# Talking-heads attention: one two-bank PSUM tile for a period's two pre-mixes, and one VectorE maximum over both

## Chip, cores and metric

The kernel runs on one core of one Trainium2 chip. The metric is device time in microseconds (us), from the start of the program to its end. Shown are the median of three runs of the kernel before, and one more execution that was profiled.

## What is computed

Three stages follow each other: an attention in which the heads are mixed before and after the softmax, and two feed-forward layers. The change lies in the attention.

```python
# q, k, v: 4 batches, 12 heads, 448 tokens, head size 64
scores = scale * np.matmul(q, k.transpose(0, 1, 3, 2))
scores = np.einsum('bhij,hg->bgij', scores, w_pre)          # pre-mix of the heads
scores = scores - np.max(scores, axis=-1, keepdims=True)
attn = np.exp(scores)
attn = attn / (np.sum(attn, axis=-1, keepdims=True) + 1e-09)
attn = np.einsum('bhij,hg->bgij', attn, w_post)             # post-mix of the heads
attn_out = np.matmul(attn, v)
# then two feed-forward layers over 1792 tokens: 768 -> 1024 -> 768 and 768 -> 2048 -> 768
```

## The kernel before

**Blocks and periods.** The queries of each batch are cut into chunks of 120 or 88 tokens, and each chunk into blocks of up to ten queries. A block holds its queries times twelve heads on the partitions and the 448 keys along the free dimension. There are 180 blocks; two neighbours make a period, so there are 90 periods, `s` = 0 to 89.

**The way of one block.** `qk` (line L222) makes scores with TensorE, in a ring of PSUM tiles of two banks each (two buffers), and ScalarE copies them to an SBUF tile `ssrc` (L229). `shuffle` (L236) is a DMA that gathers a block's rows into `sdst`. `pre` (L256) mixes the heads: per period two blocks, each into a PSUM tile of its own of one bank (`ps_pre`, four buffers: two periods' worth). `negmax` (L267) lets VectorE find the negated maximum of each row, per block. `expo` (L274) lets ScalarE compute the exponential with that maximum as bias, per block, and its row sum into `sm`. `weigh` (L284, L285, L287) is three GpSimd operations for a period: reciprocals of the sums, multiplied into the post-mix weights `w`. `post` (L307) mixes and transposes with TensorE into the same ring as `qk`; `post_out` (L337) copies that to `at` with VectorE. `av` (L373) multiplies by V into the ring, and ScalarE copies it out (L379, L391, L394).

**The order.** It is written out by hand: a loop over `s` issues in each step `pre(s+2)`, `post_out(s-1)`, the `qk` jobs of the step, `negmax` and then `expo` of period `s+2`, the `av` jobs, `weigh(s+1)`, and `post(s)`. Every engine runs its share strictly in that order. Between them stands the narrowing of the first layer's weights, spread over all engines (L82 to L103, L440). In the last steps of the attention no `qk` is left, and the loop instead begins to load the first layer's weights (`wraw`, three buffers), which ScalarE rounds (L477) and from which GpSimd takes the remainder (L478). The first layer's products (L490) follow.

Of the kernel before, what the change touches and what calls it, by code (L numbers as in the profile page):

```python
# [7 lines left out]
F32 = mybir.dt.float32  # L8
# [3 lines left out]
AF = mybir.ActivationFunctionType  # L12
ALU = mybir.AluOpType
AX = mybir.AxisListType
# [4 lines left out]
def kernel(  # L19
# [16 lines left out]
    nc = tc.nc  # L36
    B, D, _ = qT.shape
    H = w_pre.shape[0]
    S = v.shape[1]
# [15 lines left out]
    scale = 1.0 / float(D) ** 0.5  # L55
# [65 lines left out]
    late_p = late.__enter__()  # L121
# [111 lines left out]
    def shuffle(t):  # L233
        c, f, nk, r, oa = blocks[t]
        d = gaps[t % 10]
        (nc.scalar if t % 2 and t < 12 else nc.sync).dma_start(out=d[4:4 + r * H], in_=ssrc[c][f:f + (r - 1) * nk + 1:nk])  # L236
        sdst[t] = d

    def size(t, g):

        return RH if g == 0 else blocks[t][3] - RH

    es = {}
    sms = {}
    pres = {}
    nms = {}
    ws = {}

    def pre(s):

        ps = [psb_p.tile([128, 512], F32, tag="pre", name="ps_pre", bufs=4) for b in range(2)]
        ds = [sdst.pop(2 * s + b) for b in range(2)]
        for b, r in ((0, 0), (0, 1), (1, 0), (1, 1)):
            u = r ^ b
            m = H * size(2 * s + b, 1) if r else 64
            nc.tensor.matmul(  # L256
                out=ps[b][64 * u:64 * u + 64, 0:S],
                lhsT=wpre_bd[64 * r:64 * r + m],
                rhs=ds[b][64 * r:64 * r + m],
                start=True,  # L260
                stop=True,
            )
        pres[s] = ps

    def negmax(s, b):
        nm = late_p.tile([128, 1], F32, tag="nm", name="nm", bufs=6)
        nc.vector.tensor_reduce(out=nm, in_=pres[s][b][:, 0:S], op=ALU.max, axis=AX.X, negate=True)  # L267
        nms[s, b] = nm

    def expo(s, b):  # L270
        e = late_p.tile([128, S], F32, tag="e", name="e", bufs=6)
        if b == 0:
            sms[s] = late_p.tile([128, 2], F32, tag="sm", name="sm", bufs=4)
        nc.scalar.activation(  # L274
            out=e, in_=pres[s][b][:, 0:S], func=AF.Exp, bias=nms.pop((s, b)), scale=1.0, accum_out=sms[s][:, b:b + 1]
        )
        es[s, b] = e
        if b:
            pres.pop(s)

    def weigh(s):

        sm = sms.pop(s)
        nc.gpsimd.tensor_scalar(out=sm, in0=sm, scalar1=1e-9, scalar2=None, op0=ALU.add)  # L284
        nc.gpsimd.tensor_tensor(out=sm, in0=sm, in1=eps_sb[:, 2:3].to_broadcast([128, 2]), op=ALU.pow)  # L285
        w = late_p.tile([128, 2, H, RH], F32, tag="w", name="w", bufs=3)
        nc.gpsimd.tensor_tensor(  # L287
            out=w.rearrange("p b g i -> p b (g i)"),
            in0=wpost_bd.rearrange("p g i -> p (g i)").unsqueeze(1).to_broadcast([128, 2, H * RH]),
            in1=sm.unsqueeze(2).to_broadcast([128, 2, H * RH]),  # L290
            op=ALU.mult,
        )
        ws[s] = w
# [31 lines left out]
    def post_out(s):  # L325
        pv = pps.pop(s)[:, :, 0:NU * RH].rearrange("p u (n i) -> p u n i", i=RH)
        (c0, _, _, _, k0), (c1, _, _, _, k1) = [blocks[2 * s + b] for b in range(2)]
        for c in (c0, c1):
            if c not in at:
                at[c] = late_p.tile([128, NU, PH], F32, tag="at", name="at", bufs=2)  # L330
                nk = sorted(chunks[c]["nks"])
                if nk[0] != nk[1]:
                    t = at[c].rearrange("p n (u x) -> p n u x", u=2)
                    nc.vector.memset(t[:, :, :, RH * nk[0]:RH * nk[1]], 0.0)
        def put(c, k, h, n0, n1):
            dst = at[c][h, n0:n1].rearrange("p n (u x) -> p u n x", u=2)
            nc.vector.tensor_copy(dst[:, :, :, RH * k:RH * k + RH], pv[h, :, n0:n1])  # L337

        if c0 == c1:
            assert k0 == k1  # L340
            put(c0, k0, slice(0, 128), 0, NU)
        else:
            for b, (c, k) in enumerate(((c0, k0), (c1, k1))):
                put(c, k, slice(0, 128), b * NJ * H, b * NJ * H + NJ * H)
                put(c, k, slice(64 * b, 64 * b + 64), 2 * NJ * H, NU)
# [70 lines left out]
    def load_w1(i):  # L416
        src, dst, k, o = w1pieces[i]
        t = raw_p.tile([128, WP], I64, tag="w1raw", name="w1raw", bufs=7)
        nc.gpsimd.dma_start(out=t, in_=src[k * 128:(k + 1) * 128, o:o + WP])
        w1raw[i] = t  # L420
# [10 lines left out]
    def start_w1(i):  # L431
        part = narrow_w1(i)
        next(part)
        fill.append(part)
# [69 lines left out]
    def half_line(pool, n=8):  # L504

        nc.vector.memset(pool.tile([128, n], F32, name="pad"), 0.0)
# [60 lines left out]
    psb_p = psb.__enter__()  # L567


    DS, DP = 5, 2  # L570
# [6 lines left out]
    for c, ch in enumerate(chunks):  # L577
        if c:
            beg = (chunks[c - 1]["first"] + 1) // 2 - DS
            end = ch["first"] // 2 - DS  # L580
            for p in range(HP):
                rest = end - beg >= HP
                s = beg + rest + p * (end - beg - rest) // HP
# [24 lines left out]
    for s in range(lo_s, NP + 2):  # L608
        js = jobs.pop(s, [])
        for kind in (load_k, load_q, load_v, load_const):  # L610
            for f, a in js:
                if f is kind:
                    f(*a)
        if 0 <= s + DS < NP:
            shuffle(2 * (s + DS))
            shuffle(2 * (s + DS) + 1)
        ready = sorted(w1t)
        scales = sorted(w1s)
        for f, a in js:
            if f is x_out and s < NP:  # L620
                f(*a)
        if first_w1 <= s:
            room += share - moved.get(s, 0)
        while room >= 384 and owed < len(w1pieces):
            room -= 384
            owed += 1
        for _ in range(2):
            if len(w1at) < owed and len(w1at) - kept < 7:
                load_w1(len(w1at))
                w1at.append(s)  # L630
        new = 0 <= s + DP < NP
        if new:
            pre(s + DP)
        if 0 <= s - 1 < NP:
            post_out(s - 1)
        for f, a in js:
            if f is qk:
                f(*a)
        for b in range(2):
            if new:  # L640
                negmax(s + DP, b)
        for b in range(2):
            if new:
                expo(s + DP, b)
        for f, a in js:
            if f is av:
                f(*a)
        if 0 <= s + 1 < NP:
            weigh(s + 1)
        while begun < len(w1at) and w1at[begun] <= s - 3 and len(fill) + len(w1f) < 4:  # L650
            start_w1(begun)
            begun += 1
        for i in scales:
            scale_w1(i)
        for i in sorted(w1f):
            sq, t = w1f.pop(i)
            flush(sq, t)
            w1s[i] = t
        for _ in range(7 if any(f is av for f, a in js) else 0):
            filler()  # L660
        if 0 <= s < NP:
            post(s)
        if s >= NP:
            for f, a in js:
                if f is x_out:
                    f(*a, nc.scalar)
        for i in ready:
            store_w1(i)
        kept = begun - len(fill)
        if last_raw is None and kept == len(w1pieces) and not w1t and not w1s and not w1f:  # L670
            last_raw = s
            assert s < last_qk, s
            raws.__exit__(None, None, None)
            wi1 = tc.tile_pool(name="wi1", bufs=1, side="left", reuse_waits="tile")
            wi1_p = wi1.__enter__()
            half_line(wi1_p)
            prep = prep_first()
        if s == last_qk:
            early.__exit__(None, None, None)
            sspools[0].__exit__(None, None, None)  # L680
            wi1b = tc.tile_pool(name="wi1b", bufs=1, side="left", reuse_waits="tile")
            wi1b_p = wi1b.__enter__()
        if s + DP == NP - 1:
            psb.__exit__(None, None, None)
            psh = tc.tile_pool(name="psh", bufs=1, side="left", space=PSUM, reuse_waits="tile")
            psh_p = psh.__enter__()
            h10 = h1(0)
        if last_raw is not None and last_raw < s <= min(last_qk, last_raw + 3):
            next(prep)
        if s > last_qk:  # L690
            for _ in range(1 if s < NP - DS else 2):
                next(prep, None)
        if s in (NP - 2, NP - 1):
            next(h10)
            next(h10)
        if s == NP:
            run(prep)
            run(h10)
# [706 lines left out]
```

## Time and profile before

| what | value |
|---|---|
| median of three runs | 1093.68 us (1092.14 to 1096.95) |
| the profiled execution, whole / its span | 1091.86 us / 1090.1 us |
| TensorE busy, of the span | 1031.3 us (95%) |
| VectorE busy | 678.5 us (62%) |
| ScalarE busy | 561.7 us (52%) |
| GpSimd busy | 672.9 us (62%) |

The span is that of the profile, from the first instruction to the last; 1.8 us of the execution's own time lie around it. A share of busy time is a mean over stages: the attention ends near 392 us, and all else is feed-forward layers.

### The profile page before, as it was taken

Reading aid. Unit: us, or ns where it says so; the run is one execution under the profiler, and the core shown is the slowest. Engines: PE = TensorE matmul, PEld = TensorE weight load, DVE = VectorE, ACT = ScalarE, POOL = GpSimd, SP = SyncE. Lnnn points to the kernel's source line nnn. Section 1 sums busy time; section 2 is a strip of 40 time slices with the busy share of each in tenths; the row PEclk is TensorE's granted clock in tenths of the full one; section 3 lists DMA queues with packets and bytes.
Section 4 is the critical chain, followed back from the end, with each engine's and each line's share of the span. In section 5 each row is a group of like instructions: output and inputs, shape, how many; then the busy total and the mean of one; then the engine's idle time right before and its main releaser. Section 6 shows DMA issues by size and latency. Waiting matters only on the chain.

```text
span 1090.1 us, 30147 instructions
## 1 busy us (share of the span) xinstructions
PE 1031.3 (95%) x12220; PEld 884.1 (81%) x12220; DVE 678.5 (62%) x1131; ACT 561.7 (52%) x1195; POOL 672.9 (62%) x868
## 2 busy tenths in 40 slices
PE   7798887998999799999999999999999999999998
PEld 3466555665666688898999989999999999999998
DVE  2577765885776435888887435777646833444444
ACT  4677655786777435443443446344434555444432
POOL 4667986898765726656555158676535757666630
PEclk9999999999999999999999999999999999999999
DMA  8778887889765624556564646445545521111102
GB/s 230 211 213 251 250 231 224 254 244 255 221 205 178 182 71 138 175 180 200 163 200 128 216 140 189 138 143 155 185 163 194 192 102 59 58 59 59 58 29 102
DMA packets 115914, 181.06 MB, mean 166 GB/s; under 512 B 24224, under 2 KB 87200, under 8 KB 115776
## 3 DMA queue, kind: packets, MB, share of 16 engines
q1 hardware_dynamic: 100276, 127.79, 38.2%
q0 software_dynamic: 12608, 48.55, 14.8%
q10 hardware_dynamic: 2892, 2.80, 0.9%
q8 instruction: 96, 1.57, 0.6%
q14 instruction: 42, 0.34, 0.1%
HBM read 102.42 MB, written 38.14 MB: 129 GB/s over the span
## 4 chain that ended last, share of the span: by engine, by line
PE 52%; POOL 4%; issue 3%; DVE 2%; DMA 2%; ACT 1%; SPq 0%; POOLq 0%; ACTq 0%
PE ps_y L1218 19%; PE ps_h L1147 16%; PE ps_o L801 9%; PE ps_h L490 7%; POOL ti L1075 1%; DMA ra<-w2iD 1%; DMA w2oD<-nt 1%; PE ps_tr L787 1%; POOL s L1055 1%; POOL to L1083 1%; DVE st L760 0%; DVE e L757 0%; ACT e L754 0%; DVE nm L751 0%; POOL w1o L727 0%
## 5 line engine op out<-in xcount | busy, mean ns | idle before, releaser
L1218 PE MATMUL ps_y<-to,gt 128*128 128x384 f32 x1332 | 241.8, 336 | 2.6 <-POOL to L1083 1.8
L1218 PEld LDWEIGHTS ps_y<-to,gt 128*128 128x128 f32 x1332 | 233.6, 188 | 4.9 <-POOL to L1083 2.1
L1147 PE MATMUL ps_h<-xc,ti 128*128 128x448 f32 x1080 | 225.1, 362 | 0.6 <-ACT h L1163 0.6
L1147 PEld LDWEIGHTS ps_h<-xc,ti 128*128 128x128 f32 x1080 | 201.6, 188 | 13.2 <-ACT h L1163 1.0
L337 DVE COPY at<-ps_ring 128x840 f32<-128x840 f32 (+2 forms) x114 | 96.1, 854 | 100.7 <-PE ps_ring L307 100.6
L307 PEld LDWEIGHTS ps_ring<-w,e 60*64 60x64 f32 x5040 | 89.0, 136 | 64.9 <-issue 27.3
L1229 DVE TENSOR_TENSOR y<-ps_y,y 128x768 f32<-128x768 f32 x97 | 92.4, 954 | 77.9 <-PE ps_y L1218 77.2
L841 POOL TENSOR_SCALAR nt<-nt 128x256 f32<-128x256 f32 x96 | 111.6, 1163 | 46.0 <-ACT nt L840 40.1
L307 PE MATMUL ps_ring<-w,e 60*64 60x60 f32 x5040 | 98.7, 222 | 27.1 <-issue 14.1
L229 ACT COPY ssrc<-ps_ring 128x896 f32<-128x896 f32 x92 | 82.3, 908 | 81.1 <-PE ps_ring L222 70.7
L274 ACT ACTIVATE e<-ps_pre,nm 128x448 f32<-128x448 f32 x180 | 113.2, 640 | 19.2 <-DVE nm L267 18.5
L801 PE MATMUL ps_o<-zt,w1o 128*128 128x384 f32 (+1 forms) x720 | 120.6, 326 | 1.8 <-ACT o L809 1.6
L490 PE MATMUL ps_h<-w1i,xs 128*128 128x512 f32 x504 | 118.8, 393 | 0.7 <-POOL xs L741 0.6
L801 PEld LDWEIGHTS ps_o<-zt,w1o 128*128 128x128 f32 x720 | 116.9, 189 | 2.5 <-ACT o L809 1.9
L490 PEld LDWEIGHTS ps_h<-w1i,xs 128*128 128x128 f32 x504 | 94.3, 189 | 20.6 <-POOL xs L741 1.5
L1075 POOL TENSOR_TENSOR ti<-ra,ti 128x384 fp32r<-128x384 f32 x56 | 60.0, 1079 | 79.7 <-ACT ti L1074 79.0
L267 DVE TENSOR_REDUCE nm<-ps_pre 128x1 f32<-128x448 f32 x180 | 103.2, 614 | 9.6 <-PE ps_pre L256 8.9
L1160 DVE TENSOR_TENSOR gt<-h,gt 128x448 fp32r<-128x448 f32 x64 | 50.2, 785 | 90.0 <-ACT gt L1165 85.4
L222 PE MATMUL ps_ring<-k,q 64*64 64x448 f32 x752 | 95.9, 561 | 7.8 <-DMA q<-in_qT_dram 3.2
L840 ACT ACTIVATE nt<-nraw 128x256 f32<-128x256 f32 x96 | 41.0, 433 | 119.4 <-DMA w2iD<-nt 29.9
L256 PE MATMUL ps_pre<-sdst,wpre_bd 64*64 64x448 f32 (+1 forms) x720 | 91.9, 547 | 3.1 <-issue 2.8
L1083 POOL TENSOR_TENSOR to<-ro,to 128x768 fp32r<-128x768 f32 x32 | 61.1, 1916 | 45.7 <-ACT to L1082 45.1
(111 smaller groups left out, 1526.3 us busy)
## 6 DMA issues: line engine op xcount, KB each, us to landing
sdst<-ssrc SPq DMA_DIRECT2D x166, 210.0 KB
nraw<-in_moe_w_in_dram SPq DMA_DIRECT2D x48, 256.0 KB
nraw<-in_moe_w_out_dram SPq DMA_DIRECT2D x48, 256.0 KB
ra<-w2iD POOLq DMA_DIRECT2D x32, 384.0 KB, 4.5
ro<-w2oD POOLq DMA_DIRECT2D x32, 384.0 KB, 4.0
w1raw<-in_moe_w_in_dram POOLq DMA_DIRECT2D x24, 256.0 KB, 6.5
w1raw<-in_moe_w_out_dram POOLq DMA_DIRECT2D x24, 256.0 KB, 6.9
w2iD<-nt SPq DMA_DIRECT2D x48, 128.0 KB
```

The lines of the kernel that those rows point to most:

```text
L222: nc.tensor.matmul(out=ps[64 * u:64 * u + 64, e, 0:S], lhsT=qq[c][64 * e:64 * e + 64, p * n + u * half:p * n + u * half + 64], rhs=k[64 * ...
L256: nc.tensor.matmul(out=ps[b][64 * u:64 * u + 64, 0:S], lhsT=wpre_bd[64 * r:64 * r + m], rhs=ds[b][64 * r:64 * r + m], start=True, stop=True,)
L267: nc.vector.tensor_reduce(out=nm, in_=pres[s][b][:, 0:S], op=ALU.max, axis=AX.X, negate=True)
L274: nc.scalar.activation(out=e, in_=pres[s][b][:, 0:S], func=AF.Exp, bias=nms.pop((s, b)), scale=1.0, accum_out=sms[s][:, b:b + 1])
L307: nc.tensor.matmul(out=ps[64 * c:64 * c + 64, u, i0:i0 + PR], lhsT=ee[b][64 * u:64 * u + m, o:o + 64], rhs=w[64 * u:64 * u + m, b], start= ...
L337: nc.vector.tensor_copy(dst[:, :, :, RH * k:RH * k + RH], pv[h, :, n0:n1])
L490: nc.tensor.matmul(out=ps[:, u], lhsT=t[:, a, cc], rhs=w1i[cc][:, w, u * 512:(u + 1) * 512], start=(cc == 0 and a == 0 and w == 0), stop=( ...
L801: nc.tensor.matmul(out=ps[:, 0:width], lhsT=w1o[k][:, w, cc * 128:(cc + 1) * 128], rhs=zT[:, a, k, 0:width], start=(k == 0 and i == 0), st ...
L841: nc.gpsimd.tensor_scalar(out=t, in0=t, scalar1=2.0**-30, scalar2=2.0 - 2.0**-23, op0=ALU.is_ge, op1=ALU.mult)
L1147: nc.tensor.matmul(out=bank[b][:, 0:HT], lhsT=t[:, w, c], rhs=xc[xn][:, a, c], start=(first and j == 0 and c == 0 and i == 0), stop=(j == ...
L1218: nc.tensor.matmul(out=ps[:, u - u2[0], 0:DM // 2], lhsT=gt[:, a, f, o:o + 128], rhs=w[:, v, f, u * (DM // 2):(u + 1) * (DM // 2)], start= ...
L1229: nc.vector.tensor_tensor(out=yo, in0=po, in1=yo, op=ALU.add)
```

## The change

The two pre-mix results of a period go into one tile of two banks, in a pool of two such tiles instead of four of one bank. One VectorE operation reduces both banks, to a tile of two columns, and each exponential takes its column. The matmuls, the exponentials and all other operations stay as they are and in the same places.

```diff
-        ps = [psb_p.tile([128, 512], F32, tag="pre", name="ps_pre", bufs=4) for b in range(2)]
+        ps = psb_p.tile([128, 2, 512], F32, tag="pre", name="ps_pre", bufs=2)
...
-                out=ps[b][64 * u:64 * u + 64, 0:S],
+                out=ps[64 * u:64 * u + 64, b, 0:S],
...
-    def negmax(s, b):
-        nm = late_p.tile([128, 1], F32, tag="nm", name="nm", bufs=6)
-        nc.vector.tensor_reduce(out=nm, in_=pres[s][b][:, 0:S], op=ALU.max, axis=AX.X, negate=True)
-        nms[s, b] = nm
+    def negmax(s):
+        nm = late_p.tile([128, 2], F32, tag="nm", name="nm", bufs=4)
+        nc.vector.tensor_reduce(out=nm, in_=pres[s][:, :, 0:S], op=ALU.max, axis=AX.X, negate=True)
+        nms[s] = nm
...
-            out=e, in_=pres[s][b][:, 0:S], func=AF.Exp, bias=nms.pop((s, b)), scale=1.0, accum_out=sms[s][:, b:b + 1]
+            out=e, in_=pres[s][:, b, 0:S], func=AF.Exp, bias=nms[s][:, b:b + 1], scale=1.0, accum_out=sms[s][:, b:b + 1]
...
-        for b in range(2):
-            if new:
-                negmax(s + DP, b)
+        if new:
+            negmax(s + DP)
```

No instruction changes its place; what each waits for does. On ScalarE, in the middle of the attention, a step before the change reads (`e` is the exponential's output, the names in brackets are the engines and DMA queues waited for):

```order
L229 COPY ssrc<-ps_ring 128x2x448 [waits PE_49]
L274 ACTIVATE e,sm<-ps_pre,nm 128x448 [waits DVE_49,Pool_49]
L274 ACTIVATE e,sm<-ps_pre,nm 128x448 [waits DVE_49]
L379 COPY xt<-ps_ring 128x3x2x6x5 [waits PE_49]
L379 COPY xt<-ps_ring 128x3x2x6x5
```

and after it, in such a step:

```order
L229 COPY ssrc<-ps_ring 128x2x448 [waits PE_49]
L274 ACTIVATE e,sm<-ps_pre,nm 128x448 [waits DVE_49,Activation_49,Pool_49]
L274 ACTIVATE e,sm<-ps_pre,nm 128x448 [waits Activation_49]
L380 COPY xt<-ps_ring 128x3x2x6x5 [waits PE_49]
L380 COPY xt<-ps_ring 128x3x2x6x5
```

The second exponential no longer waits for VectorE, and the first waits for the one operation that gives both maxima. Each also names ScalarE's own earlier exponential in the same of six `e` buffers, three periods back.

On TensorE, at the pre-mix of the third period (`sdst_102` and `sdst_103` are its two blocks), the first that takes PSUM a second time, the difference is:

```order
-L256 MATMUL ps_pre<-sdst_102,wpre_bd 64x448 [waits DMAHW5_49,PE_49,Activation_49]
+L256 MATMUL ps_pre<-sdst_102,wpre_bd 64x448 [waits DMAHW5_49,DVE_49,Activation_49]
 L256 MATMUL ps_pre<-sdst_102,wpre_bd 64x448
-L256 MATMUL ps_pre<-sdst_103,wpre_bd 64x448 [waits DMAHW0_49,PE_49,Activation_49]
+L256 MATMUL ps_pre<-sdst_103,wpre_bd 64x448 [waits DMAHW0_49]
 L256 MATMUL ps_pre<-sdst_103,wpre_bd 64x448
```

The first block's matmul now waits for both exponentials of two periods before, where each block waited for its own.

## Rows read from the trace of the kernel before

**Rows 1.** Busy us of each engine in two stretches, (x) instructions.

```profile
core 0: us, PE busy (x) PEld busy (x) DVE busy (x) ACT busy (x) POOL busy (x), PEclk, DMA share, GB/s
20.00:344.00 324.00, 287.01 (x7407) 192.22 (x7399) 227.78 (x410) 223.70 (x545) 241.82 (x437) 0.98 0.78 229
392.00:1090.00 698.00, 688.95 (x3725) 652.94 (x3724) 425.77 (x679) 309.33 (x583) 392.17 (x360) 1.00 0.43 136
```

**Rows 2.** What TensorE waited for, 20 to 392 us: total us, times, longest us.

```profile
PE ps_ring L307 <- issue: 14.1, 10, 3.1
PE ps_ring L307 <- POOL w L287: 10.4, 10, 3.6
PE ps_ring L373 <- ACT ssrc L229: 10.4, 4, 3.8
...
PE ps_ring L222 <- DVE at L337: 2.5, 3, 1.6
```

**Rows 3.** Groups, 0 to 400 us: count | busy us, mean ns | idle before, releasers.

```profile
L267 DVE TENSOR_REDUCE nm<-ps_pre 128x1 f32<-128x448 f32 x180 | 103.2, 614 | 9.6 <-PE ps_pre L256 8.9 <-issue 0.2
...
L229 DVE COPY ssrc<-ps_ring 128x896 f32<-128x896 f32 x2 | 2.2, 1092 | 9.9 <-PE ps_ring L222 9.9
...
L751 DVE TENSOR_REDUCE nm<-ps_h 128x1 f32<-128x1024 f32 x1 | 1.2, 1224 | 12.1 <-DMA xD<-xt 12.1
```

**Rows 4.** What ScalarE waited for, 20 to 392 us.

```profile
ACT e L274 <- DVE nm L267: 18.5, 16, 2.9
...
ACT ssrc L229 <- DMA sdst<-ssrc: 5.8, 2, 3.5
```

**Rows 5.** What VectorE waited for, 20 to 392 us.

```profile
DVE nm L267 <- PE ps_pre L256: 8.9, 6, 4.2
```

**Rows 6.** Timeline of a quick period: start us, us, instruction, [idle before, releaser].

```profile
102.20 0.94 PE L256 MATMUL ps_pre<-sdst,wpre_bd 64*64 64x448 f32 x8
...
103.40 1.15 DVE L267 TENSOR_REDUCE nm<-ps_pre 128x1 f32<-128x448 f32 x2
...
103.96 0.91 ACT L229 COPY ssrc<-ps_ring 128x896 f32<-128x896 f32 x1 [1.67 <-PE ps_ring L222]
...
104.76 0.64 ACT L274 ACTIVATE e<-ps_pre,nm 128x448 f32<-128x448 f32 x1
...
106.84 0.99 PE L256 MATMUL ps_pre<-sdst,wpre_bd 64*64 64x448 f32 x8
```

**Rows 7.** Timeline of the first period of a chunk, where ScalarE waits for the maximum.

```profile
303.00 1.16 DVE L267 TENSOR_REDUCE nm<-ps_pre 128x1 f32<-128x448 f32 x2
...
303.66 0.63 ACT L274 ACTIVATE e<-ps_pre,nm 128x448 f32<-128x448 f32 x1 [1.45 <-DVE nm L267]
...
305.14 0.98 PE L222 MATMUL ps_ring<-k,q 64*64 64x448 f32 x8 [0.18 <-DVE at L337]
305.22 1.89 ACT L229 COPY ssrc<-ps_ring 128x896 f32<-128x896 f32 x2
...
306.17 0.75 PE L373 MATMUL ps_ring<-at,v 128*64 128x100 f32 x12
```

**Rows 8.** Timeline of the third period's pre-mix and the exponential before it.

```profile
23.93 0.63 ACT L274 ACTIVATE e<-ps_pre,nm 128x448 f32<-128x448 f32 x1
...
24.23 1.07 PE L256 MATMUL ps_pre<-sdst,wpre_bd 64*64 64x448 f32 x6
```

**Rows 9.** Timeline of the last steps, where the first layer's weights are rounded.

```profile
346.04 0.63 ACT L274 ACTIVATE e<-ps_pre,nm 128x448 f32<-128x448 f32 x1 [0.88 <-DVE nm L267]
...
347.27 0.61 ACT L477 CAST w1i<-wraw 128x512 fp32r<-128x512 f32 x1
...
347.96 1.28 POOL L478 TENSOR_TENSOR w1i<-wraw,w1i 128x512 fp32r<-128x512 f32 x1 [1.24 <-ACT w1i L477]
...
350.41 0.39 POOL L287 TENSOR_TENSOR w<-wpost_bd,sm 128x120 f32<-128x120 f32 x1
...
350.85 1.24 PE L307 MATMUL ps_ring<-w,e 60*64 60x60 f32 x53 [0.23 <-POOL w L287]
```

More of the change, by code (lines that the diff above doesn't have):

```diff
@@ L279, in expo @@
             pres.pop(s)
+            nms.pop(s)
     def weigh(s):
```

## The prediction

> **What bounds the kernel now.** I read the busy time by stretch first [rows 1]. From 392 us to the end TensorE is busy 688.95 of 698 us: that part has no room, and nothing of the change runs in it. It only starts earlier or later. So whatever the change does, it does to the moment at which the attention hands over. In the attention's main stretch, 20 to 344 us, TensorE is busy 287.01 of 324 us, GpSimd 241.82, VectorE 227.78 (70%), ScalarE 223.70, with the DMA engines at 0.78. No engine but TensorE is near full, and TensorE loses 37 us.
>
> The table of what TensorE waited for says where [rows 2]: 14.1 us inside the post-mix with no releaser the profile can name, 10.4 us for GpSimd's weights `w`, 10.4 us for ScalarE's copies of scores, and 2.5 us, in three waits, for VectorE's copy `at`. The reduction that the change touches does not stand there by name. It can reach TensorE in three ways: through VectorE's queue (the copy `at` behind it frees a ring buffer), through ScalarE (the exponential, behind which copies of scores free ring buffers), and through the exponential and GpSimd to `w`.
>
> **The reduction itself.** Before, 180 reductions take 103.2 us of VectorE, which is 103.2 / 90 = 1.147 us for the pair of a period; one lasts 614 ns [rows 3]. The profile has no reduction over two banks. Its nearest rows: one over 1024 elements, also out of a tile of two banks, at 1224 ns, and a copy of 896 elements out of a two-bank tile at 1092 ns [rows 3]. The line through the two reductions is (1224 - 614) / 576 = 1.059 ns an element, and gives 614 + 448 x 1.059 = 1088 ns for 896. I take 1.09 us. Bounds: 1224 x 896 / 1024 = 1.07 us from below, two single means, 1.23 us, from above, should the second row of output start afresh. VectorE is thus relieved of 1.147 - 1.09 = 0.057 us a period, 5.1 us over 90 periods; by the bounds between 6.9 us less and 7.5 us more.
>
> Where is that worth anything? Only where TensorE waits for VectorE: three waits for the copy `at` [rows 2]. Each has one reduction close in front of it, so 3 x 0.06 = **0.2 us gained**. Elsewhere VectorE's own idle time takes it; it is idle 96 of the 324 us [rows 1].
>
> **The first exponential, later.** This is the price. Before, the first exponential could start when the first block's maximum was there, 0.614 us after the pair began; now both come at 1.09 us. That is 0.48 us later, and the second exponential, 0.63 us behind the first on the same engine, moves with it. It costs only where ScalarE was standing and waiting for the maximum. In a usual period it is not: in the quick one [rows 6] the pair starts at 103.40, ScalarE is busy with the copy of scores from 103.96, and the exponential starts at 104.76 with no idle time before it. The new maximum would be there at 103.40 + 1.09 = 104.49. The cover is 0.27 us; without that copy in front, the whole 0.48 us would be paid. ScalarE waited before an exponential 16 times for the maximum [rows 4], in 16 of 90 periods. These are the first periods of chunks, in which no copy of scores stands in front, and the last steps. So 16 x 0.48 = 7.7 us of lateness on ScalarE is the ceiling, and I ask for each what stands behind the exponential.
>
> The first period of a chunk at 303 us [rows 7] is one where it passes on. The exponential moves from 303.66 to about 304.14. ScalarE then ran without a break to the copies of scores, at 305.22 for two of 0.91 us or a little more; they move to 305.70. The first frees the ring buffer that the V product at 306.17 needs; that would start near 306.61, so TensorE loses 0.44 us. I find three such places. At the other first periods ScalarE had idle time or a rounding of weights before its next copy, or GpSimd was itself the later one. Taking 0.3 us as the mean of the three, since part of each is eaten by idle time on ScalarE: **0.9 us lost**; all of it lost would be 3 x 0.44 = 1.3 us.
>
> In the last steps [rows 9] ScalarE's exponentials also wait. The exponential at 346.04 stands in front of the rounding at 347.27, that in front of GpSimd's remainder at 347.96, which waited for it, and GpSimd works on in order to `w` at 350.41, for which TensorE waits at 350.85. A lateness of 0.4 us runs right through. After it GpSimd is the one that sets the pace of these steps, so later exponentials there find it busy. I count it once: **0.4 us lost**. Were each wait of these steps counted, it would be their part of the ceiling above.
>
> **The other edits.** Both blocks must be mixed before the reduction starts. In the quick period the pre-mix ends at 102.20 + 0.94 = 103.14, before the reduction at 103.40 [rows 6], and VectorE waited for the pre-mix only 6 times [rows 5]. Half a pre-mix, 0.47 us, is the most that each can lose: 0 to 2.8 us, and I take nothing, since in those periods ScalarE is still at a copy of scores. PSUM: the next pre-mix into the same banks now waits for both exponentials of two periods before. In the quick period these end at about 104.76 + 2 x 0.63 = 106.02 and TensorE comes at 106.84 [rows 6], a margin of 0.8 us for work that is hidden. The third period of the kernel has none: its pre-mix began at 24.23 while the second exponential ran until 23.93 + 0.63 = 24.56 [rows 8]. **0.3 us lost**, once. The added wait of an exponential for ScalarE's own exponential three periods back is for something long done; if it cost 0.05 us each, that is 180 x 0.05 = 9 us of an engine with 100 us idle, mostly unseen.
>
> **Sum.** 0.9 + 0.4 + 0.3 - 0.2 = 1.4 us later. From the profiled execution, 1091.86 us (span 1090.1 and 1.8 around it), that makes 1093.3 us. The median shown is 1.8 us above that execution, so I forecast 1093.68 + 1.4 = **1095.1 us**. Measured runs lie 5 us apart, so half a per cent, 5.5 us, is about what can be told from no change.
>
> **The rivals.**
>
> *Slower: the late maximum is on the path at every wait.* Place: the 16 waits for the maximum [rows 4]. Price: 16 x 0.48 = 7.7 us, with the third period's 0.3, so 1101.7 us. It decides from some 11 passed-on waits. For it: the chain of [rows 7] has no slack at all, and the waits for `w`, 10.4 us, hang on the exponential too. Against it: in most of those waits the next copy of scores or GpSimd is later still.
>
> The Trainium skill has a rule that speaks for this rival: Perfetto Trace Analysis, section Optimizing Scalar/DVE Operations, says that grouping into larger operations helps an engine that is saturated, while for one that is not but causes bubbles elsewhere, breaking instructions up lets work finish sooner. By that rule, with VectorE at 70%, the change goes the wrong way; the trace agrees as far as the 18.5 us for which ScalarE waited for the maximum.
>
> *Faster: VectorE was the pace.* If in the stretches where the weights are narrowed VectorE's queue sets the period, its relief shows whole: 90 x 0.057 = 5.1 us, so 1088.6 us; with the lower bound of the reduction 6.9 us, 1086.8. For it: the pair, 1.15 us, is half of a quick period, (106.84 - 102.20) / 2 = 2.32 us [rows 6], and the copy `at` comes on top. Against it: TensorE waited for VectorE by name for 2.5 us only [rows 2].
>
> *The change does not relieve VectorE.* The reduction over two banks costs two singles, 1.23 us. Then nothing is gained, and the first exponential is 0.62 us late: 1.6 x 0.62 / 0.48 = 2.1 us, so 1095.8 us.
>
> *Swallowed.* TensorE's longest waits in the attention, up to 3.8 us, are for copies of scores [rows 2], and two of those copies stood behind a transfer, for 5.8 us [rows 4]. Where a transfer lands when it would have landed anyway, a loss ahead of it fits into the wait. If that takes nearly all, what is left is below 0.5 us: 1093.7 to 1094.2 us.
>
> **How the numbers follow.** Forecast 0.50, swallowed 0.20, no relief 0.09, slower 0.12, faster 0.09. Slower by over 0.5% takes nearly all of the slower rival and nothing else: 0.11. Faster by over 0.5% needs the faster rival with the lower bound or more: 0.06. Within 0.5%: 0.83. The range reaches from 1089.5, most of the way into the faster rival, to 1100.0, most of the way to the slower one.
>
> **What would show it.** The profile after should have 90 reductions near 1.09 us, some 98 us in all; waits of exponentials for the maximum still 16 or so, but near 26 us in total instead of 18.5; TensorE's wait for copies of scores up by about a microsecond; a new wait of about 0.3 us at the third pre-mix; no change from 392 us on but the shift. I am wrong if the waits for the maximum number far more than 16 (the cover of 0.27 us was too thin), if a reduction lasts 1.2 us, or if the DMA waits of the attention move by more than all of this.

## The result, and the profile after

The changed kernel takes 1104.08 us (median of 22 runs, 1097.38 to 1114.87), the kernel before, run beside it on the same chip, 1097.53 us (22 runs, 1088.75 to 1110.07). The ratio is 1.0087, 95% interval 1.0061 to 1.0112: slower by about 9.5 us, where 1.4 us had been forecast; the two medians lie 6.6 us apart. Some executions run in a slower state of the chip: the ratios leave them out, and so do the means over profiles further down, though not the table of packets (`x4_before_pe128`, `m3_rest` and `n3_before_128` were profiled in it). The profiled execution of the changed kernel took 1097.38 us (span 1095.6), 5.5 us more than that of before; it is the quickest of the 22.

First the two stretches of [rows 1], the same view and columns, of the changed kernel:

```profile
20.00:344.00 324.00, 283.61 (x7212) 187.88 (x7204) 219.51 (x324) 219.31 (x536) 240.59 (x431) 0.97 0.79 227
392.00:1090.00 698.00, 693.95 (x3847) 657.88 (x3842) 424.64 (x676) 311.23 (x591) 392.89 (x360) 1.00 0.43 135
```

From 20 to 344 us TensorE gets through 7212 matmuls where it got through 7407: the attention is behind by then. The last product with V ends at 396.6 us, before at 389.3; what follows takes 1095.6 - 396.6 = 699.0 us, before 1090.1 - 389.3 = 700.8. So in this pair of profiles the whole loss arises in the attention.

Next the reduction's group, as in [rows 3], and what ScalarE and then VectorE waited for from 20 to 392 us (us in total, times, longest), as in [rows 4, 5]:

```profile
L267 DVE TENSOR_REDUCE nm<-ps_pre 128x2 f32<-128x896 f32 x90 | 97.4, 1083 | 13.0 <-PE ps_pre L256 12.7
```

```profile
ACT e L274 <- DVE nm L267: 29.5, 16, 5.8
...
ACT ssrc L229 <- DMA sdst<-ssrc: 6.3, 2, 4.1
```

```profile
DVE nm L267 <- PE ps_pre L256: 12.7, 8, 3.3
```

In kind this is as forecast: a reduction lasts 1083 ns (1.09 us forecast), and ScalarE waits 16 times for the maximum. The size of those waits is 11.0 us more in total (29.5 for 18.5), where 7.7 us had been the ceiling. What TensorE waited for from 20 to 392 us, as in [rows 2], shows no place that would pay for 9 us either:

```profile
PE ps_ring L308 <- issue: 14.2, 10, 3.8
PE ps_ring L374 <- ACT ssrc L229: 10.8, 7, 3.3
PE ps_ring L308 <- POOL w L288: 8.6, 7, 2.8
...
PE ps_ring L308 <- ACT ssrc L229: 2.9, 8, 0.4
PE ps_ring L222 <- DMA q<-in_qT_dram: 2.0, 1, 2.0
...
PE ps_ring L222 <- DVE at L338: 0.8, 2, 0.4
PE ps_pre L256 <- DMA sdst<-ssrc: 0.8, 1, 0.8
PE ps_pre L256 <- ACT e L274: 0.6, 1, 0.6
```

The second row for copies of scores reads, before:

```profile
PE ps_ring L307 <- ACT ssrc L229: 2.1, 6, 0.4
```

So copies of scores cost TensorE 13.7 us in two rows for 12.5, the third pre-mix has its new wait (0.6 us), one load of `q` is waited for (2.0 us), and GpSimd and VectorE are waited for less. All rows together come to 45.7 us, before to 42.5. A single profile is also noisy by several us: in seven profiles of kernels in which the tiles lie as before, the attention ends between 384.7 and 394.0 us. One thing I passed over at first is the DMA queues' part of the page, cut to the attention (packets, MB, share of the time of 16 DMA engines). Queue q1 carries, among other things, the shuffles from `ssrc` to `sdst`. The kernel before, then the changed one, 20 to 344 us:

```profile
q1 hardware_dynamic: 40877, 50.84, 51.9%
```

```profile
q1 hardware_dynamic: 40429, 50.10, 52.6%
```

Fewer packets took a larger share: 0.519 x 16 x 324 us / 40877 = 65.8 ns a packet before, 0.526 x 16 x 324 us / 40429 = 67.4 ns after. And the transfers are on the path, as the chain of work through 20 to 344 us of the changed kernel shows (shares by line, then the pieces that are shuffles, with start and us):

```profile
by line: PE ps_ring L374 15.9%; PE ps_ring L308 14.6%; PE ps_pre L256 11.7%; DMA sdst<-ssrc 10.3%; PE ps_ring L222 10.2%; issue 8.2%; ACT ssrc L229 5.3%; POOL sm L286 3.1%; ACT e L274 2.9%; POOL w1sq L102 2.7%; DMA xD<-xt 1.8%; POOL w1t L10
...
19.95 6.50 DMA sdst<-ssrc
...
65.41 9.46 DMA sdst<-ssrc
...
165.77 6.74 DMA sdst<-ssrc
...
264.25 4.58 DMA sdst<-ssrc
...
282.95 6.19 DMA sdst<-ssrc
```

With the kernel before this cannot be compared: there the chain that ended last goes back to 389 us only. Of all twenty profiles it runs through this whole stretch in five; shuffles hold 33, 30, 23 and 37 us of it in four kernels with moved tiles (the changed one, `m1_two_cols`, `m4_halves`, `n7_before_nm4`), and 18 us in the one with the old places (`x4_before_pe128`).

### The profile page after: what moved, and what is told of

It reads as the page before. It is cut to its first block, busy times and chain, and to the rows that moved or that the text cites. A ratio compares the mean times of both kernels' runs of the same rounds, so it can differ in the third digit from the quotient of the medians.

```text
span 1095.6 us, 29985 instructions
## 1 busy us (share of the span) xinstructions
PE 1036.2 (95%) x12220; PEld 884.8 (81%) x12220; DVE 674.0 (62%) x1041; ACT 560.6 (51%) x1195; POOL 675.0 (62%) x868
## 3 DMA queue, kind: packets, MB, share of 16 engines
q8 instruction: 96, 1.57, 0.6%
## 4 chain that ended last, share of the span: by engine, by line
PE 72%; POOL 8%; DMA 7%; issue 6%; ACT 4%; DVE 2%; SPq 0%; ACTq 0%; POOLq 0%
PE ps_y L1218 19%; PE ps_h L1147 16%; PE ps_o L801 10%; PE ps_h L491 8%; PE ps_ring L374 6%; PE ps_ring L308 5%; PE ps_pre L256 4%; PE ps_ring L222 4%; DMA sdst<-ssrc 3%; ACT ssrc L229 2%; POOL sm L286 1%; POOL ti L1075 1%; ACT e L274 1%; DMA ra<-w2iD 1%; DMA xD<-xt 1%
## 5 line engine op out<-in xcount | busy, mean ns | idle before, releaser
L1229 DVE TENSOR_TENSOR y<-ps_y,y 128x768 f32<-128x768 f32 x97 | 92.3, 954 | 78.4 <-PE ps_y L1218 78.0
L274 ACT ACTIVATE e<-ps_pre,nm 128x448 f32<-128x448 f32 x180 | 113.3, 641 | 29.9 <-DVE nm L267 29.5
L308 PE MATMUL ps_ring<-w,e 60*64 60x60 f32 x5040 | 99.4, 222 | 26.8 <-issue 14.2
L229 ACT COPY ssrc<-ps_ring 128x896 f32<-128x896 f32 x92 | 81.8, 909 | 78.3 <-PE ps_ring L222 68.2
L267 DVE TENSOR_REDUCE nm<-ps_pre 128x2 f32<-128x896 f32 x90 | 97.4, 1083 | 13.0 <-PE ps_pre L256 12.7
L256 PE MATMUL ps_pre<-sdst,wpre_bd 64*64 64x448 f32 x720 | 93.2, 550 | 4.7 <-issue 3.2
L374 PE MATMUL ps_ring<-at,v 128*64 128x120 f32 (+1 forms) x1152 | 79.1, 274 | 10.8 <-ACT ssrc L229 10.8
```

Source lines behind the costliest of these rows:

```text
L229: (nc.vector.tensor_copy if dve else nc.scalar.copy)(ssrc[c][:, p:H:HP, :], ps[:, :, 0:S])
L256: nc.tensor.matmul(out=ps[64 * u:64 * u + 64, b, 0:S], lhsT=wpre_bd[64 * r:64 * r + m], rhs=ds[b][64 * r:64 * r + m], start=True, stop=True,)
L267: nc.vector.tensor_reduce(out=nm, in_=pres[s][:, :, 0:S], op=ALU.max, axis=AX.X, negate=True)
L274: nc.scalar.activation(out=e, in_=pres[s][:, b, 0:S], func=AF.Exp, bias=nms[s][:, b:b + 1], scale=1.0, accum_out=sms[s][:, b:b + 1])
L308: nc.tensor.matmul(out=ps[64 * c:64 * c + 64, u, i0:i0 + PR], lhsT=ee[b][64 * u:64 * u + m, o:o + 64], rhs=w[64 * u:64 * u + m, b], start= ...
L374: nc.tensor.matmul(out=out, lhsT=lhsT, rhs=rhs, start=(j == 0), stop=(j == NJ and b == 1))
```

## The experiments

Eighteen kernels ran, each against the kernel before on the same chip, five rounds each. The first eight looked for the cause among the engines; their expectations name the theories by letters: L, the late first exponential; P, the coupling of two blocks in PSUM; W, ScalarE's added waits for itself; F, the places in the program at which TensorE fetches its instructions; D, VectorE's fewer instructions.

**Lateness and PSUM without the one reduction.** `e2_late_only` is the kernel before with the second block's maximum first, so that the first exponential waits for both:

```diff
-        for b in range(2):
+        for b in (1, 0):
             if new:
                 negmax(s + DP, b)
```

> The kernel before, with the two maxima of a period taken in the other order: the second block's first. Tiles, reductions and sizes stay. The first exponential then waits for the second reduction of the pair (1.15 us instead of 0.61 after the pair begins). Theory L (the late first exponential costs what the change cost, 1.0087): 1.006 to 1.011, and ScalarE's waits for the maximum near 27 us instead of 18.5. Theory P (the shared PSUM tile, freed only after both exponentials, is the cost): within 0.003 of 1.

Ratio 0.9982 (0.9948 to 1.0017). ScalarE's wait for the maximum rises from 18.5 [rows 4] to 21.1 us (27 had been expected), and the time does not. `e1p_swap` is the kernel before with the two PSUM tiles of a period exchanged in every second pair of periods, so that, as in the changed kernel, the first block's pre-mix waits for the second exponential of two periods before:

```diff
         ps = [psb_p.tile([128, 512], F32, tag="pre", name="ps_pre", bufs=4) for b in range(2)]
+        if s // 2 % 2:
+            ps = ps[::-1]
```

> The kernel before with four one-bank tiles, but in every other pair of periods the two blocks swap banks, so that the first block's pre-mix waits for the second exponential of two periods before, as in the changed kernel. Nothing else moves. Theory P: 1.005 to 1.010, with TensorE waiting at the third pre-mix and elsewhere. Theory L: at most 1.002 (0.3 us at the third period and little else).

1.0002 (0.9966 to 1.0039). `e1_tile_only` is the changed kernel with the shared PSUM tile but with two reductions to two tiles, `nm` as before:

```diff
-        nm = late_p.tile([128, 2], F32, tag="nm", name="nm", bufs=4)
-        nc.vector.tensor_reduce(out=nm, in_=pres[s][:, :, 0:S], op=ALU.max, axis=AX.X, negate=True)
+        nm = late_p.tile([128, 1], F32, tag="nm", name="nm", bufs=6)
+        nc.vector.tensor_reduce(out=nm, in_=pres[s][:, b, 0:S], op=ALU.max, axis=AX.X, negate=True)
...
```

> The changed kernel with two reductions again, one for each bank of the shared tile, and separate maxima. In this program the first exponential still waits for both reductions. So it has the shared tile and the late exponential (1.15 us) but not the single operation. If the single operation is worth something (theory V: VectorE relieved of 5 us and of half its waits), 1.010 to 1.015; if not, as the change, 1.006 to 1.011. Theory that only the single operation's own form costs: 1.000 to 1.003.

0.9986 (0.9953 to 1.002). What ScalarE waited for the maximum, 20 to 392 us, in `e2_late_only` and then in `e1_tile_only`:

```profile
ACT e L274 <- DVE nm L267: 21.1, 14, 2.6
```

```profile
ACT e L274 <- DVE nm L267: 23.9, 17, 2.4
```

P falls. L loses most of its ground; but both kernels wait less than the changed one (29.5 us), and what excludes it in full comes with `n1_after_nm6` and `n8_after_pad64` below.

**The other engines' instructions.** `e3_nm3` is the changed kernel with three buffers of `nm` for four, which takes ScalarE's wait for itself away from the first exponentials:

```diff
-        nm = late_p.tile([128, 2], F32, tag="nm", name="nm", bufs=4)
+        nm = late_p.tile([128, 2], F32, tag="nm", name="nm", bufs=3)
```

> The changed kernel with three buffers instead of four for the maxima. The first exponential then names two engines in its wait instead of three, since the reduction itself waits for ScalarE. Theory W (ScalarE's added waits cost): 1.000 to 1.005. Theories L and P: as the change, 1.006 to 1.011.

1.0084 (1.0049 to 1.012): W falls. `x1_after_dve_pad` adds a small fill behind each reduction of the changed kernel, so that VectorE again has two instructions a period; `x2_after_pe64` and `x3_after_pe128` add 64 and 128 TensorE instructions at the start of it (32 and 64 tiny products, 128 x 8, each with its weight load), `x4_before_pe128` adds 128 to the kernel before. The edits of `x1_after_dve_pad`, and of `x3_after_pe128` and `x4_before_pe128`:

```diff
         nms[s] = nm
+        nc.vector.memset(late_p.tile([128, 1], F32, tag="pad", name="vpad", bufs=1), 0.0)
```

```diff
     warm(12)
+    ps = spare()
+    for _ in range(64):
+        nc.tensor.matmul(out=ps[:, 0, 0:8], lhsT=wz[:, 0:128], rhs=wz[:, 0:8], start=True, stop=True)
```

> The changed kernel with one tiny VectorE operation (a memset of one column) behind each reduction: 90 instructions back on VectorE, some 6 us of its time; TensorE's program stays as in the changed kernel. Theory F (the change moved the places in TensorE's program at which TensorE runs out of instructions until a 16 KB fetch lands): as the change, 1.006 to 1.011. Theory D (fewer instructions on VectorE, or its two operations coming closer, is the cost): 1.000 to 1.004.

> The changed kernel with 32 tiny matmuls behind the warm-up at the start: 64 instructions more ahead of everything on TensorE (a fetch brings 256), about 2 us of TensorE at a time when it waits for the first loads. Theory F: another time than the change's 1.0087, by 0.004 or more either way. Theory D: as the change, up to 0.002 more.

> The same with 64 tiny matmuls: 128 instructions, half a fetch. Theory F: another time than the change's, by 0.004 or more either way. Theory D: 1.007 to 1.013.

> The kernel before with the same 64 tiny matmuls, 128 instructions. Theory F: the kernel before stands at a place of its own too, so 0.004 or more away from 1, most likely slower. Theory D: 1.000 to 1.003.

In this order 1.0097 (1.0061 to 1.0133), 1.0116 (1.0075 to 1.0157), 1.0095 (1.0057 to 1.0134) and 0.9978 (0.9941 to 1.0016). D falls: its two instructions a period do not take the loss away. F falls: no ratio moves by the 0.004 that it asked for. What was left between the slower kernels and `e1_tile_only` seemed to be the one reduction over two banks, or the tile of two columns.

**Taking the one reduction apart.** Four kernels keep the changed kernel's `nm` and vary the operation. `m1_two_cols` has two reductions of one bank that write the two columns; `m2_some` keeps the one reduction only where a copy of scores stands in front of it (70 of 90 periods), `m3_rest` only in the other 20; `m4_halves` has two reductions, each over half the columns of both banks.

```diff
-        nc.vector.tensor_reduce(out=nm, in_=pres[s][:, :, 0:S], op=ALU.max, axis=AX.X, negate=True)
+        for b in (slice(0, 2),) if both else (slice(0, 1), slice(1, 2)):
+            nc.vector.tensor_reduce(
+                out=nm[:, b], in_=pres[s][:, b, 0:S], op=ALU.max, axis=AX.X, negate=True
+            )
...
```

Here `both` is false throughout for `m1_two_cols`. For `m4_halves`, whose tile of maxima is 128 x 2 x 2 and whose exponentials take the first half's column:

```diff
-        nc.vector.tensor_reduce(out=nm, in_=pres[s][:, :, 0:S], op=ALU.max, axis=AX.X, negate=True)
+        for h in range(2):
+            nc.vector.tensor_reduce(
+                out=nm[:, h], in_=pres[s][:, :, S // 2 * h:S // 2 * (h + 1)], op=ALU.max, axis=AX.X, negate=True
+            )
...
```

> The changed kernel with its one reduction taken apart: two reductions of 448 columns, each of one bank, write the two columns of the one shared 128x2 tile of maxima. Everything else (two-bank PSUM tile, shared tile of maxima, its columns as biases of the exponentials, VectorE's wait for its own earlier work at the reduction) is as in the changed kernel. Theory Op (the one instruction over both banks is what costs): same as before, ratio 0.997 to 1.003, because this kernel has none. Theory Columns (the shared tile of maxima and the waits that it brings cost): 1.007 to 1.012 as in the changed kernel.

> The changed kernel with the one reduction only in periods in which a copy of scores stands right in front of it on VectorE; in the others two reductions of one bank each write the two columns. Theory Op: a part of the loss, in proportion to how many of the 90 periods keep the one reduction, so between 1.001 and 1.008; if the loss comes where VectorE is crowded, all of it here, 1.007 to 1.012. Theory Columns: 1.007 to 1.012.

> The complement of the kernel before it: the one reduction only in periods without a copy of scores in front of it. Theory Op: the rest of the loss, so that the two ratios less one add up to about 0.009; if the loss comes where VectorE is crowded, none here, 0.997 to 1.003. Theory Columns: 1.007 to 1.012.

> The changed kernel with two reductions for a period's one, each over half the columns of both blocks (2 x 224, both banks), so two short operations that each read both banks. The shift of the softmax is then the maximum over the first half of the columns alone, which leaves the kernel's other instructions and sizes as they are. Theory Op by its banks (an operation that reads two banks costs, whatever its length): 1.007 to 1.012. Theory Op by its length (one uninterrupted 1.08 us instead of two of 0.57 us): same as before, 0.997 to 1.003. Theory Columns: 1.007 to 1.012.

In this order 1.0097 (1.0051 to 1.0143), 1.0114 (1.0075 to 1.0152), 1.0093 (1.0048 to 1.0138) and 1.0147 (1.0078 to 1.0216). The loss does not follow the number of merged periods, and `m1_two_cols`, which has no merged reduction at all, has it whole. Its group of the reduction reads as that of before in [rows 3]:

```profile
L268 DVE TENSOR_REDUCE nm<-ps_pre 128x1 f32<-128x448 f32 x180 | 103.2, 615 | 15.2 <-PE ps_pre L256 15.0
```

So the operation is not the cause, and Theory Op falls. What all slower kernels share is a number in the line above it: four buffers of `nm` (three and five slots in `e3_nm3` and `x1_after_dve_pad`), and what all others share is six. In the compiled programs each buffer of such a small tile takes 32 bytes of a partition. Six become four, and the tiles stacked behind them move by 64 bytes, while all others stay. `sdst0` goes from 122112 = 477 x 256 to 122176, the two `ssrc` from 79104 = 309 x 256 and 100608 = 393 x 256 by the same 64, and `k`, `q` and V's tiles with them. Before, every source and destination row of a shuffle, 1792 = 7 x 256 bytes long, began on a multiple of 256.

**The place of the tiles.** `n1_after_nm6` is the changed kernel with the old amount of space; nothing else moves:

```diff
-        nm = late_p.tile([128, 2], F32, tag="nm", name="nm", bufs=4)
+        nm = late_p.tile([128, 2], F32, tag="nm", name="nm", bufs=6)
```

> The changed kernel with six buffers of the maxima for four, so that the pool takes the 192 bytes that it took before and every other tile lies where it lay in the kernel before. Theory Place (the loss is the 64-byte move of the shuffles' tiles): the loss is gone, ratio 0.997 to 1.003, low clock stretches in the attention worth 5 to 14 us as before, 1792-byte packets back to 88 to 90 ns from 94. Theory Columns (the shared tile of maxima and its waits): 1.007 to 1.012, packets without meaning.

0.9999 (0.9965 to 1.0034): the loss is gone, though the one reduction, the tile of two columns and the late exponential are all there. Theory Columns falls with it. The rival that six buffers of maxima are needed is excluded by `n8_after_pad64`, which keeps four and fills the space beside them:

```diff
         nms[s] = nm
+        if s == 0:
+            nc.vector.memset(late_p.tile([128, 16], F32, name="shift"), 0.0)
```

> The changed kernel with its four buffers of the maxima, and one 64-byte tile allocated beside them (filled once), so that every tile from v down lies where it lay in the kernel before. Theory Place: 0.997 to 1.003, the packets of 1792 bytes at 88 to 90 ns. Theory Buffers (four buffers of the shared maxima are too few, six are enough): 1.007 to 1.012.

1.0021 (0.9987 to 1.0054). ScalarE's waits for the maximum in `n1_after_nm6`, then in `n8_after_pad64` (which has two more lines ahead of the exponential), show the lateness whole, without the loss; so L falls:

```profile
ACT e L274 <- DVE nm L267: 25.9, 15, 4.3
```

```profile
ACT e L276 <- DVE nm L267: 27.7, 16, 4.6
```

And `n7_before_nm4` is the kernel before, two tiles and two reductions, with two buffers of `nm` fewer:

```diff
-        nm = late_p.tile([128, 1], F32, tag="nm", name="nm", bufs=6)
+        nm = late_p.tile([128, 1], F32, tag="nm", name="nm", bufs=4)
```

> The kernel before with four buffers of the maxima for six and nothing else: two tiles, two reductions, and the addresses of the changed kernel for every tile from v down. Theory Place: 1.007 to 1.012 and packets of 1792 bytes at 92 to 94 ns, without any part of the change in the code that runs. Theory Columns, and the change itself as the cause: 0.997 to 1.003. (Theory Buffers could also make it slower, by waits of VectorE for ScalarE in front of the reductions, which the trace would show.)

1.0072 (1.0042 to 1.0102): the loss without the change. The queue's row, 20 to 344 us, and behind it the row of busy times as in [rows 1], of `n1_after_nm6`:

```profile
q1 hardware_dynamic: 40871, 50.82, 51.6%
```

```profile
20.00:344.00 324.00, 285.89 (x7336) 192.52 (x7332) 222.39 (x326) 222.89 (x543) 243.70 (x437) 0.97 0.78 229
```

the same of `n8_after_pad64`:

```profile
q1 hardware_dynamic: 40843, 50.79, 51.9%
```

```profile
20.00:344.00 324.00, 285.03 (x7288) 190.68 (x7288) 221.47 (x326) 222.21 (x542) 241.71 (x436) 0.97 0.78 229
```

and of `n7_before_nm4`, with the shuffles' pieces in its chain of work:

```profile
q1 hardware_dynamic: 40197, 49.72, 52.9%
```

```profile
20.00:344.00 324.00, 280.47 (x7131) 190.50 (x7132) 222.19 (x400) 216.52 (x527) 235.30 (x425) 0.96 0.80 226
```

```profile
65.16 10.32 DMA sdst<-ssrc
...
164.97 9.72 DMA sdst<-ssrc
...
262.76 6.31 DMA sdst<-ssrc
...
284.94 5.70 DMA sdst<-ssrc
...
307.71 4.82 DMA sdst<-ssrc
```

Per packet that is 65.4, 65.9 and 68.2 ns: with the old places the queue is as quick as before, with the moved ones it is slow again, and the DMA engines are busier (0.80 for 0.78) to move less (226 GB/s for 229).

**Other distances.** Three kernels leave the change out and move `sdst`, `ssrc`, `q` and `k` by padding of 64, 128 and 256 bytes; `v` and the small tiles stay:

```diff
     gaps = [late_p.tile([128, S], F32, name=f"sdst{i}") for i in range(10)]
+    nc.vector.memset(late_p.tile([128, 16], F32, name="shift"), 0.0)
```

> The kernel before, with nothing of the change, and 64 bytes of padding that move the shuffles' sources and destinations, q and k by 64 bytes (one small memset at the start is added). Theory Place: as slow as the changed kernel, 1.007 to 1.012, 1792-byte packets at 92 to 94 ns. Theory Columns: same as before, 0.997 to 1.003.

> As the kernel before it, moved by 128 bytes. If multiples of 128 are enough, same as before, 0.997 to 1.003, packets 88 to 90 ns. If it takes multiples of 256 (the Trainium skill, DMA: Bandwidth & Descriptors, section How a descriptor splits into AXI transactions, splits a descriptor at them), 1.007 to 1.015 and packets at 92 ns or more. Theory Columns: 0.997 to 1.003.

> As the two before it, moved by 256 bytes: the same move of tiles and the same added memset, but back on multiples of 256. Theory Place: same as before, 0.997 to 1.003, packets 88 to 90 ns; if it were the padding or the memset as such, 1.007 to 1.012. Theory Columns: 0.997 to 1.003.

1.0043 (1.0004 to 1.0082), 0.9986 (0.9948 to 1.0025) and 0.9969 (0.993 to 1.0007). Below are all kernels by where the first byte of `sdst0` lies behind a multiple of 256. The packets are the 1792-byte ones of q1 that start between 20 and 344 us, some 18,000 to 19,600 in each, averaged from the trace's records; they are the shuffles' alone:

| kernel | bytes behind 256 | mean packet, ns | ratio |
|---|---|---|---|
| before | 0 | 89.6 | 1 |
| e1_tile_only, e1p_swap, e2_late_only, x4_before_pe128 | 0 | 88.3, 89.5, 89.2, 90.4 | 0.9986, 1.0002, 0.9982, 0.9978 |
| n1_after_nm6, n8_after_pad64, n4_before_256 | 0 | 88.9, 89.5, 87.9 | 0.9999, 1.0021, 0.9969 |
| x1_after_dve_pad | 32 | 93.0 | 1.0097 |
| changed, x2_after_pe64, x3_after_pe128, m1_two_cols | 64 | 93.3, 93.9, 93.2, 92.2 | 1.0087, 1.0116, 1.0095, 1.0097 |
| m2_some, m3_rest, m4_halves, n7_before_nm4 | 64 | 93.8, 92.3, 93.2, 95.1 | 1.0114, 1.0093, 1.0147, 1.0072 |
| e3_nm3 | 96 | 93.2 | 1.0084 |
| n3_before_128 | 128 | 92.5 | 0.9986 |
| n2_before_64 | 192 | 93.7 | 1.0043 |

The mean packets split without overlap: 87.9 to 90.4 ns on multiples of 256, 92.2 to 95.1 off them. The shortest ones do not: 74 ns is the most frequent time in all twenty profiles. What differs is how many packets take no longer than that: 62 to 68% at 0 bytes, 35% at 32, 37 to 45% at 64, 48% at 96, 54% at 128, 42% at 192.

The times follow with an exception. At 128 the mean packet is slow and the time is not longer, and at 192 it is longer by half as much, with an interval that holds the whole loss too. So a slower mean packet does not by itself bring the loss. Whether the smaller set of tiles moved there (V's stay) or the distance itself makes the difference stays open.

## Why the prediction was wrong

**The step that failed** is the part on the other edits. It costs both blocks' mixing, PSUM and the added wait, and says nothing of `bufs=6` becoming `bufs=4`, which stands in the diff beside the reduction; so that edit stood in the sum at zero, without a reason, with every other tile taken as unmoved. It is the edit that costs, by the places of the other tiles: with the old places the change runs at 0.9999 and 1.0021, and the edit alone makes the kernel before slower, at 1.0072. No rival had a price for it. The last sentence named waits for transfers as a sign of being wrong, but it would hardly have told: from 20 to 392 us ScalarE's wait for shuffles went from 5.8 [rows 4] to 6.3 us, TensorE's waits for transfers from 0.2 to 2.8, of which 2.0 are one load of `q`; and in `n7_before_nm4`, which has the loss, no row has TensorE wait for a transfer. The time per packet told.

**How 64 bytes become 9 us** is shown in part only. The place of the tiles is the cause; that it works through the shuffles is argued. For it: the mean packet is slower by 4%, and the chain passes through shuffles for 33.5 us from 20 to 344 us (the five pieces above). TensorE's own work does not suffer by the move: outside the stretches at the low clock, 20 to 340 us, a product with V takes 247.6 ns before and 247.2 after, a matmul of the pre-mix 541.5 and 541.2; and the packets of V's loads, 6144 bytes, take 357 and 345 ns. Against it: 4% of 33.5 us is 1.3 us, far from 9, and `n3_before_128` has slow packets without a loss.

TensorE waits more, and its clock adds to that. In the attention the granted clock falls to 0.5, the 1.2 GHz level, for some microseconds at a time. One such stretch of the changed kernel, with what lies ahead of it and behind it (columns as in [rows 1]):

```profile
36.50:46.70 10.20, 7.36 (x217) 4.49 (x209) 6.20 (x7) 8.18 (x20) 6.82 (x15) 1.00 0.70 209
46.70:53.50 6.80, 5.06 (x62) 3.67 (x64) 2.12 (x2) 1.31 (x4) 2.59 (x6) 0.50 0.91 217
53.50:63.70 10.20, 8.69 (x248) 6.09 (x248) 4.31 (x5) 5.00 (x11) 4.10 (x9) 1.00 0.79 203
```

TensorE had stood still from 44.68 to 48.44 us (the 3.8 us of the first row of its waits); at the low clock it does 62 matmuls in 5.06 us of work. From the start to the end of the last product with V, TensorE stood idle for 44 to 53 us, mean 49.1, in the seven profiles with the old places, and for 47 to 61, mean 54.2, in the ten with moved ones. It ran at the low clock for 7 to 24 us, mean 18.1, against 24 to 38, mean 30.4 (stretches that begin after 20 us). The 12.3 us more at half speed do the work of 6.2, so, as an estimate, at most 6.2 us are lost there (part of the time TensorE is idle in them, which then counts twice). With 5.1 us more idle time that covers the 11.3 us by which the attention ended later on the mean (401.0 for 389.7 us; two of the ten also have the added products at the start). That a slower shuffle lengthens just those gaps was not shown gap by gap: the more idle time is spread over waits for copies, for instructions and for transfers.

**The other steps held, as far as they can be told.** The reduction: 1083 ns for 1.09 us. The waits for the maximum with the old places (`n1_after_nm6`, `n8_after_pad64`): 15 and 16 for 16, 25.9 and 27.7 us for 26. The third pre-mix: 0.6 us in the changed kernel and 0.8 in those two for 0.3, mis-sized by a factor of two to three. The 0.05 us for an exponential's added wait came from no row; `e3_nm3`, whose first exponentials do not have that wait, ran at 1.0084, and `n1_after_nm6`, whose have it, at 0.9999. The later part of the program: 699.0 us for 700.8. The sum of 1.4 us, 1.0013, lies between the two restored kernels' ratios, whose intervals hold both it and no change at all; so the terms' sizes, 0.9 us among them, were not tested.

**The rivals.** "Slower: the late maximum" gave 1101.7 us, 1.0073, close to the measured ratio by luck: `n1_after_nm6` and `n8_after_pad64` have the late maximum whole, and their intervals end at 1.0034 and 1.0054. So the rule of the Trainium skill that spoke for it (Perfetto Trace Analysis, section Optimizing Scalar/DVE Operations) had no effect here that could be measured, one way or the other. "Faster: VectorE was the pace" would have made these two kernels 0.995; their intervals begin at 0.9965 and 0.9987. "The change does not relieve VectorE" falls with the 1083 ns, for 1.23 us. "Swallowed", at most 1.0005, lies in both intervals like the forecast, and stays open.

No version beats the kernel before beyond its interval.

## What to carry to other kernels

Read `bufs`, shapes and tags in a diff also as addresses: a few bytes of a tiny tile move everything stacked behind it, and rows that a DMA reads or writes may lose a boundary on which they began, here of 256 bytes, without a word of the change being about them. When experiments that undo the visible edits do not move the loss, compare where the tiles lie, and try the bare move on the unchanged kernel. Padding the small tile back costs 64 bytes and separates the edit from its side effect in one run.

## What the runs showed of the hardware

- **SBUF-to-SBUF packets of 1792 bytes** take on the mean 4% longer off multiples of 256 bytes (92.2 to 95.1 ns for 87.9 to 90.4), and for the mean the distance hardly matters: 93.0 at 32 bytes, 93.2 at 96, 92.5 at 128, 93.7 at 192. The most frequent time stays 74 ns; fewer packets keep to it (35 to 54% for 62 to 68%). The Trainium skill, DMA: Bandwidth & Descriptors, section How a descriptor splits into AXI transactions, says that a descriptor is cut at multiples of 256 bytes, and that one which begins off them starts with a transaction from the boundary below, whose first bytes are fetched for nothing. By that page 1792 bytes are, as an estimate, 7 transactions on a boundary and 8 off it, whatever the distance, and 56 beats of 32 bytes against 57 (at 32 bytes) to 62 (at 192). The traces agree that 256 is the boundary (128 is not enough for the mean packet, by one profile); the price is smaller than one transaction in seven, and does not grow as the beats would.
- **Instruction fetches** interrupt TensorE, by all that these traces show. In the gap of 3.8 us above, a transfer of 16384 bytes on the instruction queue runs from 45.88 to 46.95 us, and TensorE resumes 1.49 us later; in the kernel before, gaps that end at 46.02 and 53.88 us have such transfers that end at 44.53 and 52.31 us, 1.49 and 1.57 us earlier. In both profiles each gap of over 1 us from 20 us to the attention's end for which the view names no releaser, seven in either, ends 1.3 to 1.6 us behind such a transfer. These gaps are not the loss: those inside the post-mix come to 14.2 us, before to 14.1 [rows 2]. Adding 64 or 128 instructions ahead, which moves their places in the program, changed no time beyond the intervals (`x2_after_pe64`, `x3_after_pe128`, `x4_before_pe128`).
